# A fused top-k attention and GELU MLP: the last rows' turned probabilities go through VectorE and DRAM, their products with v move later, and the small loads of v change queue

## The chip, the cores and the metric

The kernel runs on one core of a Trainium2 chip. The metric is the device time of one execution in microseconds (us). Three runs of the kernel before took 1480.41, 1480.58 and 1481.08 us (median 1480.58). Engines are named as in the profile: PE (TensorE matmul), PEld (its weight loads), DVE (VectorE), ACT (ScalarE), POOL (GpSimd), SP (SyncE, which here only issues DMAs).

## The reference

Eight batches, eight heads, 576 rows, head size 64, float32. Every row of scores keeps its 32 largest entries; softmax over those; product with v. The heads side by side form x (4608 tokens by 512), and an MLP with an exact GELU follows.

```python
scores = scale * np.matmul(q, k.transpose(0, 1, 3, 2))
kth = np.partition(scores, -top_k, axis=-1)[..., -top_k:-top_k + 1]
scores = np.where(scores >= kth, scores, -1000000000.0)
attn = np.exp(scores - np.max(scores, axis=-1, keepdims=True))
attn = attn / (np.sum(attn, axis=-1, keepdims=True) + 1e-09)
x = np.matmul(attn, v)                      # (B,H,S,D), then to (B*S, H*D)
h = x @ w_in
out = (0.5 * h * (1.0 + erf(h / sqrt(2)))) @ w_out
```

## The kernel before

**Items.** Heads are taken in pairs. An item is 128 rows of scores for both heads of a pair: a tile `s` of 128 partitions and 1152 columns (two heads of 576). A head has 576 = 4 x 128 + 64 rows, so four full row tiles (t = 0 to 3) and 64 last rows (t = 4, `NM`). An item of last rows takes 64 rows of two heads of two pairs. A batch has 16 full items and two of last rows; even batches put their last rows behind their full items, odd batches before them. So four items of last rows stand together at each border between an even and an odd batch: items 16 to 19, 52 to 55, 88 to 91 and 124 to 127 of 144.

**Slots.** The loop `for n in range(ahead)` (L1154) writes the order of every engine out by hand. In slot n: the scores of items n+2 and n+3 on PE in even slots (L386, L401) and their copies from PSUM by ACT (L394, L406); the scores against the last 64 keys, "keys", one item a slot (L349, L363, copied by ACT at L357, L369); the 32 largest of item n on DVE (`top_k`, L483, L486); the selection and the exponentials of item n-1 on ACT (`softmax`, L517, L529), its sum (L510, POOL), reciprocal (L504, DVE, the last DVE instruction of the slot) and scaling (L552, POOL); the turning of P, the scaled probabilities, of item n-2; and the product with v (`attend`) of item n-3 at the slot's start on PE, whose result ACT copies to `xT` (L720 for full items, L731 for last rows). Between these `mlp` puts pieces of the MLP on PE: first-layer pieces (`h_ps`, L773) in even slots, second-layer pieces (`seven`, L927, and `y_ps`, L929) in odd slots, after the GELU (L789) of the pieces before. The GELU and the exponentials use different tables, so an odd slot has two table loads on ACT.

**Two ways to turn P.** On PE: `tails` (L622 for last rows, L619 for others) and `both` (eight transposes, L649) into PSUM, then ACT copies (L635 twice for last rows, L629 for others; L664). Or, for items where `squared(i)` holds (48 even full items): DVE turns all 32 x 32 squares in place in the middle of `top_k` (`square_p`, L569), SP writes the tile to DRAM with four DMAs at the end of the slot (`write_p`, L579), and at the start of the next slot SP reads it back, rearranged, with four DMAs into the left half of `pt` (`read_p`, L586) once the writes have landed.

**Buffers and waits.** `pt`, the turned P of two items side by side, is one buffer. The score tile `s` has six buffers, so item i+6 takes that of item i once the turning has read it. From slot START + 3 on (START is 10) every `bank(...)` is the same single PSUM bank "z": `o` (the product with v), `seven` and the keys use it in turn, and each must wait for the ACT copy of the one before. All loads and stores of the main part go through SP, in order; `issue` holds loads of v back behind `write_p` when the slot has one. In the built program each DMA gets one of eight completion semaphores in turn, whichever queue issues it, and the issuing engine first waits until the DMA that had this semaphore last has landed.

The loads of v of the next batch (`load("v", ...)`, L737) follow the product of the items that used the buffers last: each pair has two loads of 128 KB over 128 partitions (L131) and two of 16 KB over 64 partitions (L134).

Of the kernel before, what the change touches and what calls it, by code (L numbers as in the profile page):

```python
# [14 lines left out]
def kernel(  # L15
# [30 lines left out]
    NP = H // 2  # L46
    NM = S // P
# [51 lines left out]
    def issue(f):  # L99

        if held[0]:
            late_issues.append(f)
        else:
            f()
# [232 lines left out]
    def halves(t, e, step):  # L337

        return spread(t[:, e * TL :], step + (TL if e == 0 else -TL), TL)

    def pair_tile(name, tag="pr"):
        return ps.tile([P, 2, 512], f32, tag=tag, bufs=1, name=name)

    def last_keys(i, t_ps):

        pair, t = items[i]
        s = S_of[i]
        if t < NM:
            nc.tensor.matmul(  # L349
                t_ps[:, 0:P], lhsT=q_of[pair][:, t * P : (t + 1) * P],  # L350
                rhs=kt_of[pair][:, SM : SM + P], start=True, stop=True,
            )
# [4 lines left out]
            return lambda: nc.scalar.activation(  # L357
                s[:, SM : S + TL], t_ps[:, 0:P], func=AF.Copy, scale=scale
            )
        for r in range(2):  # L360
            kt = kt_of[pair + r]
            for e in range(2):
                nc.tensor.matmul(  # L363
                    t_ps[half(r, e), r * TL : (r + 1) * TL],
                    lhsT=kt[:, SM + P + e * TL : SM + P + (e + 1) * TL],
                    rhs=kt[:, SM + e * TL : SM + (e + 1) * TL],
                    start=True, stop=True,
                )
        return lambda: nc.scalar.activation(  # L369
            s.rearrange("p (r n) -> p r n", r=2)[:, :, SM:S],  # L370
            t_ps[:, 0:P].rearrange("p (r n) -> p r n", r=2), func=AF.Copy, scale=scale,
        )

    def scores(i, second=False):
        if i >= N or i in S_of:
            return
        pair, t = items[i]
        S_of[i] = s = work.tile([P, 2 * S], f32, tag="s", bufs=6, name="s")
        s_ps = pair_tile("s_ps", "l1" if second else "pr")
        if not few[0]:  # L380
            last_keys(i, bank("t_ps"))()
        if t < NM:
            q_t, kt = q_of[pair][:, t * P : (t + 1) * P], kt_of[pair]
            for e in range(2):
                rows = slice(e * D, (e + 1) * D)
                nc.tensor.matmul(  # L386
                    s_ps[:, e], lhsT=q_t[rows, :], rhs=kt[rows, 0:SM], start=True, stop=True
                )
            if i == 0:

                nc.scalar.activation(s[:, 0:SM], s_ps[:, 0], func=AF.Copy, scale=scale)
                nc.scalar.activation(s[:, S + TL :], s_ps[:, 1], func=AF.Copy, scale=scale)  # L392
                return
            nc.scalar.activation(spread(s, S + TL, SM), s_ps, func=AF.Copy, scale=scale)  # L394
        else:

            for r in range(2):
                kt = kt_of[pair + r]
                for e in range(2):
                    rows = slice(e * D, (e + 1) * D)  # L400
                    nc.tensor.matmul(  # L401
                        s_ps[half(r, e), r, :], lhsT=kt[rows, SM + P + e * TL : SM + P + (e + 1) * TL],
                        rhs=kt[rows, 0:SM], start=True, stop=True,
                    )
            s2 = s.rearrange("p (r n) -> p r n", r=2)
            nc.scalar.activation(s2[:, :, 0:SM], s_ps, func=AF.Copy, scale=scale)  # L406

    lists_of = {}
    HS = S // 2
# [171 lines left out]
    def read_p(i):  # L581

        if squared(i):
            d = turned.pop(i)
            for k in range(P // SQ):
                nc.sync.dma_start(  # L586
                    out=pt_now[0][k * SQ : (k + 1) * SQ, :, 0:P], in_=d[:, :, k, :]
                )

    def transposes(i):  # L590
# [3 lines left out]
        if squared(i):  # L594

            def keys_only(ahead):
                pt_now[0] = work.tile([P, 2 * NM + 1, 2 * P], f32, tag="pt", bufs=1, name="pt")
# [7 lines left out]
        def tails(ahead):  # L605
            tp = bank("tp_t")
            keys = last_keys(ahead, tp) if ahead is not None and ahead < N else None
            at = P
            if t % 2 == 0:
                pt_now[0] = work.tile([P, 2 * NM + 1, 2 * P], f32, tag="pt", bufs=1, name="pt")  # L610
            if diag is not None:
                for e in range(2):
                    nc.tensor.matmul(
                        tp[e * TL : (e + 1) * TL, at : at + P],
                        lhsT=s[:, SM + e * TL : SM + (e + 1) * TL], rhs=diag[:, e],
                        start=True, stop=True,
                    )
            elif t < NM:
                nc.tensor.transpose(tp[:, at : at + P], s[:, SM : S + TL], ident)  # L619
            else:  # L620
                for r in range(2):
                    nc.tensor.transpose(  # L622
                        tp[0:TL, at + r * P : at + (r + 1) * P],
                        s[:, r * S + SM : (r + 1) * S], ident,
                    )
            if keys:
                keys()
            if t < NM:
                nc.scalar.copy(  # L629
                    out=pt_now[0][:, NM, t % 2 * P : (t % 2 + 1) * P], in_=tp[:, at : at + P]  # L630
                )
                return
            for e in range(2):
                c = slice(e * TL, (e + 1) * TL)
                nc.scalar.copy(  # L635
                    out=halves(pt_end[c, 0, :], e, P),
                    in_=halves(tp[0:TL, at : at + 2 * P], e, P),
                )

        x = t % 2 * P if t < NM else 0  # L640

        def turn_over(tp, e):
            first = e * (S + TL if t < NM else S)
            for j in range(NM):
                to, part = tp[:, j * P : (j + 1) * P], s[:, first + j * P : first + (j + 1) * P]
                if diag is not None:
                    nc.tensor.matmul(to, lhsT=part, rhs=diag[:, e], start=True, stop=True)
                else:
                    nc.tensor.transpose(to, part, ident)  # L649
# [33 lines left out]
    def copy_x():  # L683
        while copies:
            copies.pop()()
# [10 lines left out]
    def attend(i):  # L696
# [24 lines left out]
        else:  # L721
            for r in range(2):
                vt = raw_of("v", pair + r)
                for j in range(NJ):
                    for e in range(2):
                        nc.tensor.matmul(
                            o[e * D : (e + 1) * D, r * TL : (r + 1) * TL], lhsT=vt[:, j, e, :],
                            rhs=pt[:, r * NJ + j, half(r, e)] if j < NM else pt_end[:, r, half(r, e)],
                            start=(j == 0), stop=(j == NJ - 1),
                        )  # L730
            copies.append(lambda: nc.scalar.copy(  # L731
# [588 lines left out]
```

## Time and profile before

| | us |
|---|---|
| median of three runs | 1480.58 |
| the profiled execution's own time | 1479.73 |
| its span in the profile | 1478.0 |
| PE busy | 1461.6 |
| DVE busy | 1294.3 |
| POOL busy | 1140.1 |
| ACT busy | 1099.9 |

Busy times are sums over the whole span, and say little on a single slot: with 144 items in 1478.0 us a slot takes about 10 us, and its limit changes from slot to slot. Slots are best cut at the reciprocal (L504) that ends a slot on DVE. In the profile a matmul in float32 shows as two instructions, so "x8" is four matmuls of the program, and successive start times tell more of PE than busy times do, since matmuls overlap.

### The profile page before, as it was taken

The numbers are of one execution on the slowest core, as the hardware profiler recorded it, in microseconds if no ns is written. First come the engines' busy times: TensorE is split into PE (matmuls) and PEld (weight loads), VectorE is DVE, ScalarE is ACT, GpSimd is POOL, SyncE is SP. The second block draws the span as 40 slices with busy tenths as digits, with TensorE's granted clock in tenths as the row PEclk, the third lists the DMA queues.
The fourth block names the chain that finished last, engine by engine and source line by source line (L and its number), as shares of the span: only waits on it lengthen the run. The fifth ranks groups of instructions, "written<-read, shape, count | busy, mean of one in ns | idle before, by whom it ended". The sixth has DMA issues, their size and how long they took to land. (4 is left out here: it accounts for less than half of the span.)

```text
span 1478.0 us, 27006 instructions
## 1 busy us (share of the span) xinstructions
PE 1461.6 (99%) x8817; PEld 1147.9 (78%) x8817; DVE 1294.3 (88%) x3318; ACT 1099.9 (74%) x1942; POOL 1140.1 (77%) x1291
## 2 busy tenths in 40 slices
PE   8999999999999999999999999999999999999999
PEld 6876677877777777887777778787777777787787
DVE  8999899999999988999999987999999997998701
ACT  7999977877777687777777778777777777776620
POOL 6877567877898879877898978886788887987732
PEclk9999999999999999999999999999999999999999
DMA  7424310045435322345534331345453421233300
GB/s 198 143 86 124 84 48 1 24 88 101 95 73 93 66 58 52 65 95 108 105 83 81 69 61 47 66 93 99 97 103 73 89 55 41 61 61 72 70 15 15
DMA packets 477645, 112.94 MB, mean 76 GB/s; under 512 B 413216, under 2 KB 469056, under 8 KB 477504
## 3 DMA queue, kind: packets, MB, share of 16 engines
q1 hardware_dynamic: 476240, 110.78, 35.3%
q8 instruction: 70, 1.15, 0.3%
q14 instruction: 71, 0.58, 0.1%
q10 hardware_dynamic: 1200, 0.39, 0.1%
q0 software_dynamic: 64, 0.03, 0.0%
HBM read 73.39 MB, written 37.75 MB: 75 GB/s over the span
## 5 line engine op out<-in xcount | busy, mean ns | idle before, releaser
L773 PE MATMUL h_ps<-xT,w_in_sb 128*128 128x256 f32 (+1 forms) x2560 | 536.2, 361 | 0.1
L773 PEld LDWEIGHTS h_ps<-xT,w_in_sb 128*128 128x128 f32 x2560 | 436.5, 190 | 73.4 <-issue 25.2
L483 DVE MAX8 top<-lists 128x8 f32<-128x576 f32 (+1 forms) x792 | 476.4, 641 | 0.0
L486 DVE MATCH_REPLACE8 lists<-top,lists 128x288 f32<-128x288 f32 (+1 forms) x528 | 307.9, 589 | 0.0
L552 POOL TENSOR_TENSOR s<-s,rden 128x1152 f32<-128x1152 f32 x135 | 285.8, 2117 | 0.3 <-DVE rden L504 0.3
L529 ACT ACTIVATE s<-s,bias 128x576 f32<-128x576 f32 x288 | 225.4, 787 | 11.0 <-issue 0.4
L517 ACT ACTIVATE s<-s,neg 128x576 f32<-128x576 f32 x288 | 225.5, 793 | 1.7 <-POOL neg L497 1.6
L510 POOL TENSOR_SCALAR den<-den 128x2 f32<-128x2 f32 x144 | 31.4, 218 | 215.9 <-ACT s L529 210.2
L455 POOL TENSOR_TENSOR lists<-lists 128x576 int32<-128x576 int32 x132 | 186.2, 1410 | 4.0
L447 POOL TENSOR_TENSOR lists<-s 128x576 int32<-128x576 int32 x133 | 187.2, 1407 | 0.0
L715 PE MATMUL o<-pt,raw_v 128*64 128x256 f32 x1280 | 153.0, 384 | 1.8 <-ACT s L529 1.1
L715 PEld LDWEIGHTS o<-pt,raw_v 128*64 128x64 f32 x1280 | 87.8, 136 | 85.8 <-issue 37.2
L789 ACT ACTIVATE g<-h_ps 128x512 f32<-128x512 f32 x144 | 78.2, 594 | 100.6 <-PE h_ps L773 100.4
L929 PE MATMUL y_ps<-w_out_sb,sum 128*128 128x256 f32 x472 | 140.4, 379 | 0.0
L394 ACT ACTIVATE s<-s_ps 128x1024 f32<-128x1024 f32 x127 | 125.5, 1035 | 10.5 <-PE s_ps L386 10.3
L664 ACT COPY pt<-tp 128x1024 f32<-128x1024 f32 x85 | 86.6, 1019 | 62.2 <-PE tp L649 62.1
L386 PE MATMUL s_ps<-kt,qm 64*128 64x512 f32 x512 | 129.4, 618 | 0.8 <-ACT s L392 0.8
L504 DVE RECIPROCAL rden<-den 128x2 f32<-128x2 f32 x144 | 23.2, 161 | 108.6 <-POOL den L510 107.4
L486 DVE MATCH_REPLACE8 lists<-first,lists 128x288 f32<-128x288 f32 x264 | 114.3, 439 | 0.0
L929 PE MATMUL y_ps<-w_out_sb,g 128*128 128x256 f32 x480 | 113.4, 379 | 0.0
L483 DVE MAX8 first<-lists 128x8 f32<-128x288 f32 x268 | 106.6, 436 | 0.0
L929 PEld LDWEIGHTS y_ps<-w_out_sb,g 128*128 128x128 f32 x480 | 91.2, 190 | 12.4
(167 smaller groups left out, 2533.1 us busy)
## 6 DMA issues: line engine op xcount, KB each, us to landing
turned<-s SPq DMA_DIRECT2D x192, 144.0 KB, 3.5
pt<-turned SPq DMA_DIRECT2D x192, 144.0 KB, 3.2
raw_v<-in_v_dram SPq DMA_DIRECT2D x64, 128.0 KB, 2.4
out_dram<-y SPq DMA_DIRECT2D x30, 256.0 KB, 2.1
raw_q<-in_q_dram SPq DMA_DIRECT2D x112, 64.0 KB, 2.0
raw_k<-in_k_dram SPq DMA_DIRECT2D x112, 64.0 KB, 2.0
w_out_sb<-in_moe_w_in_dram SPq DMA_DIRECT2D x14, 511.8 KB, 4.8
w_out_sb<-in_moe_w_out_dram SPq DMA_DIRECT2D x10, 511.8 KB, 4.1
```

The lines of the kernel that those rows point to most:

```text
L386: nc.tensor.matmul(s_ps[:, e], lhsT=q_t[rows, :], rhs=kt[rows, 0:SM], start=True, stop=True)
L394: nc.scalar.activation(spread(s, S + TL, SM), s_ps, func=AF.Copy, scale=scale)
L447: nc.gpsimd.tensor_tensor(t[:, :, 1].bitcast(i32), a.bitcast(i32), b.bitcast(i32), op=ALU.add)
L455: nc.gpsimd.tensor_tensor(into_of(i)[:, :, 1].bitcast(i32), both, top, op=ALU.subtract)
L483: nc.vector.max(x[:, e], src[:, e])
L486: nc.vector.match_replace(dst[:, e], x[:, e], src[:, e], LOWEST)
L517: nc.scalar.activation(s, s, func=AF.Prelu, bias=st["neg"][:, e : e + 1], scale=1.0, alpha=STEEP)
L529: nc.scalar.activation(s, s, func=AF.Exp, bias=st["bias"][:, e : e + 1], scale=1.0, accum_out=st["den"][:, e : e + 1],)
L552: nc.gpsimd.tensor_tensor(s, s, wide, op=ALU.mult)
L715: nc.tensor.matmul(o[e * D : (e + 1) * D, 0:n], lhsT=vt[:, j, e, :], rhs=pt[:, e * NJ + j if j < NM else NM, :], start=(j == 0), stop=(j = ...
L773: nc.tensor.matmul(h_tile(u)[:, i, :], lhsT=w_in_sb[:, ko, f * P : (f + 1) * P], rhs=xT[:, ko, c0 : c0 + n], start=(ko == 0), stop=(ko == ...
L929: nc.tensor.matmul(acc[names][:, k], lhsT=lhsT, rhs=rhs, start=(j == 0 and k == 0), stop=(j == FT // 2 - 1 and k == 1),)
```

## The change

Items of last rows beyond item 26 (52 to 55, 88 to 91, 124 to 127: twelve items) are turned by DVE squares and DRAM, like the even full items. Two such items share one `pt`, left and right half. Their tails and their heads are laid out in `s` as in a full item (both heads' last columns side by side in the middle), so that items 16 to 19, which are still turned on PE, need one transpose and one copy for the tails instead of two and two; `pt_end` goes. The product of an even item of an even batch (52) moves from the start of slot 55 to the start of slot 56; those of 53, 54 and 55 move from the starts of slots 56, 57 and 58 to the middle of slots 57, 59 and 59, ahead of the slot's keys, and `read_p` of that slot moves behind them. The two 16 KB loads of v of each pair that follow these products are issued by ACT instead of SP: eight DMAs at each border, four at the end of slot 56 and four at the end of slot 57.

```diff
         for e in range(2):
                 nc.tensor.matmul(
-                    t_ps[half(r, e), r * TL : (r + 1) * TL],
+                    t_ps[half(r, e), e * TL : (e + 1) * TL],
...
                     nc.tensor.matmul(
-                        s_ps[half(r, e), r, :], lhsT=kt[rows, SM + P + e * TL : SM + P + (e + 1) * TL],
+                        s_ps[half(r, e), e, :], lhsT=kt[rows, SM + P + e * TL : SM + P + (e + 1) * TL],
...
-            nc.scalar.activation(s2[:, :, 0:SM], s_ps, func=AF.Copy, scale=scale)
+            nc.scalar.activation(spread(s, S + TL, SM), s_ps, func=AF.Copy, scale=scale)
...
-    pt_end = const.tile([P, 2, P], f32, name="pt_end")
-    nc.gpsimd.memset(pt_end, 0.0)
 
     def squared(i):
 
-        return SINGLE.stop - 2 < i < N - 2 and i % 2 == 0 and items[i][1] < NM and i % RINGS != 12
+        if not SINGLE.stop - 2 < i < N - 2:
+            return False
+        return items[i][1] == NM or (i % 2 == 0 and i % RINGS != 12)
+
+    def delayed(i):
+
+        return squared(i) and items[i][1] == NM
+
+    def pt_tile():
+        return work.tile([P, 2 * NM + 1, 2 * P], f32, tag="pt", bufs=1, name="pt")
...
         if squared(i):
             d = turned.pop(i)
+            if i % 2 == 0:
+                pt_now[0] = pt_tile()
+            cols = slice(i % 2 * P, (i % 2 + 1) * P)
             for k in range(P // SQ):
                 nc.sync.dma_start(
-                    out=pt_now[0][k * SQ : (k + 1) * SQ, :, 0:P], in_=d[:, :, k, :]
+                    out=pt_now[0][k * SQ : (k + 1) * SQ, :, cols], in_=d[:, :, k, :]
                 )
...
-                            rhs=pt[:, r * NJ + j, half(r, e)] if j < NM else pt_end[:, r, half(r, e)],
+                            rhs=pt[:, e * NJ + j if j < NM else NM, i % 2 * P :][:, half(r, e)],
...
-                issue(lambda r=r: load("v", pair + r + NP))
+                issue(lambda r=r: load("v", pair + r + NP, None, nc.scalar if delayed(i) else None))
...
         held[0] = n < N and squared(n - 2)
-        read_p(n - 3)
+        mid = [i for i in (n - 5, n - 4) if delayed(i) and n % 2 and (i % 2 or i in starts)]
+        if not mid:
+            read_p(n - 3)
...
-        product = attend(n - 3)
+        if delayed(n - 4) and n % 2 == 0 and n - 4 not in starts:
+            product = attend(n - 4)
+        else:
+            product = not delayed(n - 3) and attend(n - 3)
...
         mlp(1)
+        if mid:
+            for i in mid:
+                attend(i)
+                copy_x()
+            read_p(n - 3)
```

More of the change, by code (lines that the diff above doesn't have):

```diff
@@ L335, in half @@
         return slice((r ^ e) * TL, ((r ^ e) + 1) * TL)
-    def halves(t, e, step):
-        return spread(t[:, e * TL :], step + (TL if e == 0 else -TL), TL)
     def pair_tile(name, tag="pr"):
@@ L369, in last_keys @@
         return lambda: nc.scalar.activation(
-            s.rearrange("p (r n) -> p r n", r=2)[:, :, SM:S],
-            t_ps[:, 0:P].rearrange("p (r n) -> p r n", r=2), func=AF.Copy, scale=scale,
+            s[:, SM : S + TL], t_ps[:, 0:P], func=AF.Copy, scale=scale
         )
@@ L401, in scores @@
                     nc.tensor.matmul(
-                        s_ps[half(r, e), r, :], lhsT=kt[rows, SM + P + e * TL : SM + P + (e + 1) * TL],
+                        s_ps[half(r, e), e, :], lhsT=kt[rows, SM + P + e * TL : SM + P + (e + 1) * TL],
                         rhs=kt[rows, 0:SM], start=True, stop=True,
                     )
-            s2 = s.rearrange("p (r n) -> p r n", r=2)
-            nc.scalar.activation(s2[:, :, 0:SM], s_ps, func=AF.Copy, scale=scale)
+            nc.scalar.activation(spread(s, S + TL, SM), s_ps, func=AF.Copy, scale=scale)
     lists_of = {}
@@ L596, in keys_only @@
             def keys_only(ahead):
-                pt_now[0] = work.tile([P, 2 * NM + 1, 2 * P], f32, tag="pt", bufs=1, name="pt")
                 if ahead is not None and ahead < N:
@@ L608, in tails @@
             at = P
-            if t % 2 == 0:
-                pt_now[0] = work.tile([P, 2 * NM + 1, 2 * P], f32, tag="pt", bufs=1, name="pt")
+            if i % 2 == 0:
+                pt_now[0] = pt_tile()
             if diag is not None:
@@ L617, in tails @@
                     )
-            elif t < NM:
+            else:
                 nc.tensor.transpose(tp[:, at : at + P], s[:, SM : S + TL], ident)
[L620 to L625, printed above, removed]
             if keys:
                 keys()
[L628 to L640, printed above, removed]
+            nc.scalar.copy(out=pt_now[0][:, NM, x : x + P], in_=tp[:, at : at + P])
+        x = i % 2 * P
         def turn_over(tp, e):
-            first = e * (S + TL if t < NM else S)
+            first = e * (S + TL)
             for j in range(NM):
@@ L1177 @@
             scores(n + 3)
-        product = attend(n - 3)
+        if delayed(n - 4) and n % 2 == 0 and n - 4 not in starts:
+            product = attend(n - 4)
+        else:
+            product = not delayed(n - 3) and attend(n - 3)
         late = n > START
```

## The prediction

> **What bounds the kernel now.** I read the page first (shares, clock), then stretches of one border cut at the reciprocals that end slots 53 to 59 (the view by windows), then the order of PE, ACT and SP in them.
>
> ```profile
> span 1478.0 us, 27006 instructions
> PE 1461.6 (99%) x8817; PEld 1147.9 (78%) x8817; DVE 1294.3 (88%) x3318; ACT 1099.9 (74%) x1942; POOL 1140.1 (77%) x1291
> PEclk9999999999999999999999999999999999999999
> ```
>
> PE looks like the bound, and its clock never falls. But PE's figure is an average over slots with other limits. The six rows below are slots 54 to 59, where the four items of last rows 52 to 55 are turned and multiplied:
>
> ```profile
> 526.70:536.76 10.06, 10.06 (x63) 8.33 (x60) 8.09 (x23) 6.63 (x13) 9.35 (x11) 1.00 0.07 11
> 536.76:549.07 12.31, 12.31 (x103) 9.53 (x102) 8.09 (x23) 10.27 (x22) 5.91 (x6) 1.00 0.22 50
> 549.07:559.34 10.27, 10.25 (x121) 9.00 (x118) 8.10 (x23) 7.05 (x15) 10.03 (x12) 1.00 0.27 60
> 559.34:569.48 10.14, 10.14 (x54) 7.76 (x53) 8.09 (x23) 9.53 (x17) 9.98 (x12) 1.00 0.14 53
> 569.48:578.75 9.27, 9.27 (x80) 8.30 (x79) 9.27 (x23) 6.62 (x13) 8.66 (x10) 1.00 0.27 42
> 578.75:587.00 8.25, 8.12 (x43) 6.34 (x43) 8.12 (x23) 6.67 (x14) 6.00 (x6) 1.00 0.44 98
> ```
>
> Columns: stretch, its length, then busy time of PE, PEld, DVE, ACT, POOL, then clock and DMA. In slots 56 and 57 POOL is busy 10.03 of 10.27 and 9.98 of 10.14 us: POOL, not PE, sets them, since its sum (L510) stands behind its other work and the reciprocal waits for it. Slot 58 is all DVE (9.27 of 9.27). Only in slots 54 and 55 are DVE (8.09) and POOL both short of the length.
>
> **The change, part by part.** PE's share, from start to start:
>
> ```profile
> 531.68 0.38 PE L622 MATMUL tp_t<-ident,s 128*64 128x128 f32 x2
> 531.89 1.03 PE L773 MATMUL h_ps<-xT,w_in_sb 128*128 128x256 f32 x4
> 532.76 1.04 PE L649 MATMUL tp<-ident,s 128*128 128x128 f32 x8
> 533.63 3.62 PE L773 MATMUL h_ps<-xT,w_in_sb 128*128 128x256 f32 x16
> 537.18 0.69 PE L726 MATMUL o<-pt,raw_v 128*64 128x64 f32 x16
> 538.50 1.13 PE L773 MATMUL h_ps<-xT,w_in_sb 128*128 128x256 f32 x4
> L569 DVE STREAM_TRANSPOSE s<-s 128x1152 f32<-128x1152 f32 x48 | 65.5, 1364 | 0.0
> ```
>
> Tails take 531.89 - 531.68 = 0.21 us, the eight transposes 533.63 - 532.76 = 0.87, one product with v 538.50 - 537.18 = 1.32. So PE is relieved of 1.08 us in each of slots 54 to 57 (4.3 us a border), and DVE gets 1.36 us in each. ACT loses the copies behind them, which hide in its idle time.
>
> Slot 54 becomes 8.09 + 1.36 = 9.45 on DVE, with the wait for POOL 9.6: 0.46 saved. Slot 55 loses its product too: ACT's chain there (10.27 busy) starts earlier and is shorter by the copies, so DVE's 9.45 to 9.5 decides: 2.81 saved. Slots 56 and 57: DVE's 9.45 and PE's smaller load hide under POOL, whose instructions stay the same, end to end up to the sum:
>
> ```profile
> 556.91 0.73 POOL L979 TENSOR_TENSOR y<-y 128x256 f32<-128x256 f32 x1
> 557.59 1.41 POOL L455 TENSOR_TENSOR lists<-lists 128x576 int32<-128x576 int32 x1
> 559.08 0.22 POOL L510 TENSOR_SCALAR den<-den 128x2 f32<-128x2 f32 x1
> ```
>
> Nothing saved there. So at most 3.27 us a border are to be had, not 4.3.
>
> Slot 59 pays. It now holds two products in a row, both in bank z: that of 54 (PE), its copy (ACT), that of 55, its copy, then the keys.
>
> ```profile
> 579.73 0.78 ACT L517 ACTIVATE s<-s,neg 128x576 f32<-128x576 f32 x1 [0.18 <-POOL neg L497]
> 580.57 1.28 ACT L529 ACT_TABLE_LOAD   x1
> 581.87 0.78 ACT L529 ACTIVATE s<-s,bias 128x576 f32<-128x576 f32 x1
> 582.64 0.26 ACT L357 ACTIVATE s<-tp_t 128x128 f32<-128x128 f32 x1
> 581.24 0.41 PEld L349 LDWEIGHTS tp_t<-kt,qm 128*128 128x128 f32 x2
> 587.00 0.17 DVE L504 RECIPROCAL rden<-den 128x2 f32<-128x2 f32 x1
> ```
>
> The first copy stands behind the selection, table load and exponential, which cannot start before slot 58's end: it comes at 582.64 - 578.75 = 3.9 us into the slot however early PE is. Then copy 0.3, product 1.4, copy 0.4: keys at 6.15 instead of 2.5. From the keys to the reciprocal are 5.76 us, 5.45 without a wait of 0.3 there. Slot 59 is then 11.4 to 11.6 instead of 8.25: at least 3.1 lost, which takes back the gain.
>
> The DMAs. Per border 16 writes and 16 reads are new on SP's queue; eight small loads leave it.
>
> ```profile
> 574.82 3.40 SPq L579 DMA_DIRECT2D turned<-s  x4
> 580.89 2.55 SPq L586 DMA_DIRECT2D pt<-turned  x4
> pt<-turned SPq DMA_DIRECT2D x192, 144.0 KB, 3.2
> raw_v<-in_v_dram SPq DMA_DIRECT2D x64, 16.0 KB, 2.3
> L134 SPq DMA_DIRECT2D raw_v<-in_v_dram x64: 465/512/1687, 23.7 to 1249.7; - x64
> L131 ACTq DMA_DIRECT2D raw_k<-in_k_dram x2: 500/525/550, 0.7 to 1.3; - x2
> SPq L134 <- DMA w_out_sb<-in_moe_w_in_dram: 1.8, 2, 1.0
> ```
>
> A write set takes 3.4 us to issue and has landed 580.89 - 574.82 = 6.05 after its first issue (the reads wait for that); a read set 2.55 and 3.2 to land. One load on ACT holds its queue 0.5 us (nearest row: 0.525 for a larger load), four 2.1. The last row shows a load of v waiting for a load it has nothing to do with: the eight semaphores in turn. Here that ties SP to ACT: in the built program the last load of v behind item 52's product takes the semaphore of ACT's first load at the end of slot 57, and the four reads of 54, next on SP, those of its others. So SP stands until ACT is at the end of slot 57, and behind SP's reads of 54 stand the writes of 55. Who waits for those: item 61 takes 55's score buffer, and its scores are copied on ACT at the start of slot 58, in front of everything that slot 58 has on ACT. (Item 59 waits likewise for 53's writes in slot 56, about 1.5 us, under POOL's cover.)
>
> From slot 57's start: exponential at 3.9, product's copy, keys and their copy to 4.7, second selection, second exponential from 5.5 to 6.5. ACT's loads go out under this exponential (5.5) or after it (6.5, and 0.5 later still by the four of slot 56, which push the GELU back). Second load landed: 0.5 + 2.3 later, 8.3; reads of 54 till 11.0; writes of 55 from there, landed 17.1. Slot 58 starts at 10.14, so ACT is held till 6.9 us into it; late end 8.5. Then copy 1.0, selection and exponential twice (1.75 each), keys' copy 0.25, sum and reciprocal 0.5: slot 58 ends at 12.2 to 13.8 instead of 9.27: 3.0 to 4.5 lost. And slot 59's ACT work then begins with the GELU that was held up (table 1.3, GELU 1.05, copy 0.25, begun 0.5 before the slot): first copy at 5.2 instead of 3.9, slot 59 about 12.6: 4.3 lost.
>
> Sum a border: -0.46 - 2.81 + 3.0 to 4.5 + 4.3 = +4.0 to +5.5; nothing in the rows places ACT's loads between these ends, so I take the middle, 4.75. Slot 60 begins as it did, so nothing is made up. Three borders: +14.2. Items 16 to 19 save one tail transpose (0.11, half of 0.21) on PE each, in slots where PE has no idle time: -0.4. The scores' new banks, same instructions: 0, bounds -0.3 and +0.3. Against the profiled execution's 1479.73: 1493.5; the median of the runs stands 0.85 above it: 1494.
>
> **A rule that bears on it.** The Trainium skill, "DMA: Bandwidth & Descriptors", section Issuing engines are not separate DMA queues, says that issuing from several engines saves only the issuing time. By the rows that is eight times 0.5 us of SP, which is not what SP waits for here.
>
> **The rivals.**
> (1) The gain stays, slower falls away: the reads of 54 go out right behind 53's product (SP not held by ACT), and PE, 1.32 us lighter in slot 58, is so far ahead that slot 59's products fit. Then 3.27 x 3 + 0.4 = 10.2 saved: 1470. For it: SP is idle most of the time. Against: the copy at 3.9 us needs DVE's slot 58. It decides if writes of 55 land before slot 58 and the keys of slot 59 come by 3.5 us.
> (2) Only slot 59 pays: -3.27 + 3.2 = 0 a border, 1480. For it: the writes of 55, free of ACT, would land about 2 us into slot 58, in time.
> (3) PE's clock falls. In this schedule PE has done slot 58's first-layer pieces about 7.2 us into the slot and then needs bank z, which the held keys' copy frees at 10.2 to 11.7: PE stands still for 3 to 4.5 us. What a low clock costs:
>
> ```profile
> L1113 PE MATMUL warm<-raw_v 128*128 128x128 f32 x18 | 4.2, 430 | 1.0 <-DVE raw_v L85 1.0
> L1113 PE MATMUL warm<-ident 128*128 128x128 f32 x276 | 32.7, 275 | 0.0
> ```
>
> The first 18 matmuls of the kernel took 430 ns, later ones 275: 1.56 times. On slot 59's path are 3.4 us of PE work (product 1.3, keys to last transpose 2.1), so +1.9 a border: 1500. No clock row of this trace has fallen, so I give it little. The Trainium skill, "TensorE: Matmul & The Clock Gate", Part 1, has the clock halved after an idle window of about 3.4 us; by that the same work would take 3.4 more a border. No run here shows it yet.
> (4) The gain of slot 55 fails (DVE waits for ACT there as now) with all else as forecast: 2.81 x 3 more, 1502.
>
> **How the numbers follow.** Chances: forecast 0.58, (1) 0.14, (2) 0.10, (3) 0.11, (4) 0.07. Time 1494, its own range 1490 to 1498. The range 1479 to 1503 leaves out (1) and a tail. About 0.2% (3 us) is what a measurement of this kernel can tell from no change. Faster 0.14, same 0.10, slower 0.76.
>
> **What the profile after would show.** Right: slots 54 and 55 at about 9.6, slots 56 and 57 unchanged; ACT idle for several us at the start of slot 58 before the scores' copy, ended by the DMA `turned<-s`; SP waiting for a load on ACT's queue before the second half of its loads of v; slots 58 and 59 at 12 to 14 us; PE idle between the two products. Wrong: slot 58 still 9.3 us (the tie of SP to ACT costs nothing), slots 56 and 57 shorter (POOL isn't their limit), or slot 59 near 8.3.

## The result and the profile after

The changed kernel takes 1493.17 us (median of four runs, 1492.42 to 1495.59) against 1480.49 for the kernel before (four runs, 1480.03 to 1481.08): 1.0088 times, interval 1.0071 to 1.0106. It is slower by 12.7 us, and the forecast was 1494 us in a range of 1479 to 1503. The profiled execution took 1492.54 us, its span is 1490.8.

Slot lengths, from reciprocal to reciprocal, in us, with the prediction's term beside the measured change (an own table, worked out from those start times; the three borders hold slots 54 to 59, 90 to 95, 126 to 131):

```
slot   before   after (borders 1, 2, 3)   change          predicted
54     10.06     9.61   9.59   9.60       -0.45 to -0.47  -0.46
55     12.31     9.27   9.27   9.27       -3.04           -2.81
56     10.27    10.49  10.50  10.50       +0.22            0
57     10.14    10.15  10.15  10.15       +0.01            0
58      9.27    12.07  11.93  12.94       +2.7 to +3.7    +3.0 to +4.5
59      8.25    12.48  12.48  12.48       +4.23           +4.3
sum                                       +3.8, +3.6, +4.6  +4.0 to +5.5
```

The same six slots of the first border in the view by windows; columns as before (stretch, length, busy time of PE, PEld, DVE, ACT, POOL, clock, DMA share, GB/s):

```profile
527.20:536.81 9.61, 9.61 (x56) 7.86 (x53) 9.35 (x23) 6.50 (x11) 9.37 (x11) 1.00 0.35 54
536.81:546.08 9.27, 9.27 (x56) 6.96 (x56) 9.27 (x23) 8.42 (x18) 5.91 (x6) 1.00 0.61 124
546.08:556.58 10.50, 10.50 (x78) 9.32 (x75) 9.39 (x25) 6.21 (x12) 10.13 (x12) 1.00 0.66 126
556.58:566.73 10.15, 8.18 (x71) 5.69 (x70) 9.35 (x24) 6.67 (x13) 9.99 (x12) 1.00 0.41 89
566.73:578.80 12.07, 8.52 (x37) 7.13 (x36) 9.35 (x24) 4.58 (x9) 8.65 (x10) 0.92 0.88 205
578.80:591.28 12.48, 11.49 (x122) 9.11 (x122) 8.09 (x23) 8.66 (x17) 5.91 (x6) 0.94 0.56 113
```

Slot 55 is now as long as DVE is busy in it. Slot 57 is still POOL's. In slot 58 no engine is busy for more than 9.35 of 12.07 us: it waits. What it waits for stands in the order of SP and ACT there (start, duration, then in brackets idle time before and what ended it; SPq and ACTq are the issues of DMAs, and "..." marks lines left out):

```profile
557.33 7.00 SPq L131 DMA_DIRECT2D raw_v<-in_v_dram  x4
564.68 3.03 SPq L590 DMA_DIRECT2D pt<-turned  x4
567.81 3.26 SPq L580 DMA_DIRECT2D turned<-s  x4
...
562.04 0.78 ACT L523 ACTIVATE s<-s,bias 128x576 f32<-128x576 f32 x1
562.05 1.12 ACTq L134 DMA_DIRECT2D raw_v<-in_v_dram  x2
...
563.21 1.25 ACTq L134 DMA_DIRECT2D raw_v<-in_v_dram  x2
...
574.08 1.03 ACT L389 ACTIVATE s<-s_ps 128x1024 f32<-128x1024 f32 x1 [8.05 <-DVE lists L480]
```

and, in the view of waits for SP over the border:

```profile
SPq L131 <- DMA raw_v<-in_v_dram: 4.6, 1, 4.6
SPq L580 <- DMA raw_v<-in_v_dram: 3.0, 1, 3.0
```

SP stands 4.6 us inside four of its own loads of v, ahead of the fourth. In the trace this load has the same completion semaphore as the load that ACT issues at 562.05, and it goes out at 563.96; the first three reads of 54 have those of ACT's other three loads. So SP reads 54 at 564.68 and writes 55 at 567.81. (The 3.0 us are the last write of 54, which waits in the same way for ACT's fourth load of slot 56; slot 57 stays as long as it was.) The writes of 55 have landed 6.2 us after the first was issued, and ACT's copy of the scores of item 61, which needs 55's score buffer, starts at 574.08, 7.35 us into the slot. The row names DVE as releaser, but that had long been done. At the second and third border the same row names the DMA, and over the whole span ACT's idle time ahead of these copies has gone from 10.5 us (all but 0.2 put down to PE) to 46.5, of which 21.0, the largest part, are put down to the writes (timeline, then the costliest groups):

```profile
1278.53 1.02 ACT L389 ACTIVATE s<-s_ps 128x1024 f32<-128x1024 f32 x1 [7.98 <-DMA turned<-s]
```

```profile
L389 ACT ACTIVATE s<-s_ps 128x1024 f32<-128x1024 f32 x127 | 125.8, 1032 | 46.5 <-DMA turned<-s 21.0
```

In slot 59 the two products and the keys wait for ACT one after the other (timeline of ACT and PE):

```profile
583.15 0.78 ACT L523 ACTIVATE s<-s,bias 128x576 f32<-128x576 f32 x1
...
583.93 0.24 ACT L718 COPY xT<-o 128x128 f32<-128x128 f32 x1
...
584.23 1.39 PE L713 MATMUL o<-pt,raw_v 128*64 128x64 f32 x40 [0.62 <-ACT xT L718]
585.98 0.49 PE L345 MATMUL tp_t<-kt,qm 128*128 128x128 f32 x2 [0.37 <-ACT xT L718]
```

The first copy comes 5.13 us into the slot, right behind the exponential, the keys 7.18 us into it.

### The profile page after: what moved, and what is told of

Its sections match the earlier page's. It is cut to its first block, busy times and chain, and to the rows that moved or that the text cites. A ratio compares the mean times of both kernels' runs of the same rounds, so it can differ in the third digit from the quotient of the medians.

```text
span 1490.8 us, 26923 instructions
## 1 busy us (share of the span) xinstructions
PE 1452.5 (97%) x8693; PEld 1136.9 (76%) x8693; DVE 1308.9 (88%) x3330; ACT 1082.9 (73%) x1902; POOL 1140.7 (77%) x1290
## 3 DMA queue, kind: packets, MB, share of 16 engines
q8 instruction: 69, 1.13, 0.3%
## 5 line engine op out<-in xcount | busy, mean ns | idle before, releaser
L389 ACT ACTIVATE s<-s_ps 128x1024 f32<-128x1024 f32 x127 | 125.8, 1032 | 46.5 <-DMA turned<-s 21.0
L651 ACT COPY pt<-tp 128x1024 f32<-128x1024 f32 x73 | 74.5, 1020 | 55.9 <-PE tp L636 55.8
```

## The experiments

In each diff, the lines not named are those of the changed kernel unless another base is given. Each comparison is with the kernel before on the same chip (medians 1480.59, 1480.63 and 1480.88 us in the three sets).

### The loads back on SP

```diff
-                issue(lambda r=r: load("v", pair + r + NP, None, nc.scalar if delayed(i) else None))
+                issue(lambda r=r: load("v", pair + r + NP))
```

> The changed kernel with one edit: the small loads of v go back to SP's queue. Tie theory (ACT's loads hold SP by the semaphores in turn, SP's late writes of 55 hold ACT in slot 58): ACT's wait at the start of slot 58 falls from 8 us to at most 2.5 us, slot 58 from 12.1 to 9.4 us, slot 59 from 12.5 to 11.5 us since its GELU is no longer late; 3 x 3.8 = 11 us less, 1482 us. Rival A (slot 59's two products alone are the loss, slot 58 is long because PE and ACT wait for P itself): slots 58 and 59 stay, 1493 us. Rival B (the halved clock is the loss): the two borders with a fall keep it if PE still stands still over 3.4 us.

1484.33 us (1483.07 to 1485.99), 1.0025 times, interval 1.0015 to 1.0035. Slot 58 is 9.27, 9.28 and 9.39 us at the three borders: the loads on ACT's queue made it long. The copy of item 61 still waits 4.73 us, but has run at 569.41, 3.3 us into the slot, under DVE's 9.28. The median is 2.3 us over the 1482 that was expected: slot 59 stays long, 12.94, 11.66 and 12.75, and slots 61, 96 and 97 grow by 0.7, 0.2 and 1.4. The three lengths of slot 59 differ by PE's clock (windows of the first and second border, then PE behind the keys of the first, and of the second):

```profile
575.39:588.33 12.94, 10.76 (x114) 8.46 (x114) 8.13 (x24) 7.43 (x16) 6.01 (x6) 0.87 0.64 134
925.67:937.33 11.66, 9.15 (x115) 7.14 (x115) 8.12 (x24) 7.81 (x17) 6.00 (x6) 1.00 0.65 131
```

```profile
581.36 0.67 PE L345 MATMUL tp_t<-kt,qm 128*128 128x128 f32 x2 [0.39 <-ACT xT L718]
...
583.74 1.63 PE L636 MATMUL tp<-ident,s 128*128 128x128 f32 x8
...
932.03 0.49 PE L345 MATMUL tp_t<-kt,qm 128*128 128x128 f32 x2 [0.39 <-ACT xT L718]
...
933.33 1.04 PE L636 MATMUL tp<-ident,s 128*128 128x128 f32 x8
```

At full clock the slot is 11.66, and the prediction's own figure for a slot 59 whose GELU isn't late was 11.4 to 11.6. Where the clock had fallen, PE took 583.74 - 581.36 = 2.38 us from the keys to the transposes instead of 933.33 - 932.03 = 1.30.

### The loads on ACT alone, in the kernel before

```diff
-                issue(lambda r=r: load("v", pair + r + NP))
+                issue(lambda r=r: load("v", pair + r + NP, None, nc.scalar if t == NM and i > 26 else None))
```

> The kernel before with one part of the change alone: the eight 16 KB loads of v of each border are issued by ACT, the turning and the products stay as they were. Theory (the tie of SP to ACT costs only because reads and writes of the last rows' P stand behind SP's loads): in the kernel before SP has nothing urgent behind them until item 56 is written in slot 58, so the tie costs nothing, and what is left is ACT's own time, 2 us in each of the two slots where the loads stand. Slot 55 (12.31 us, ACT busy 10.27) may take up to 2 us of it, slot 56 is POOL's and hides it: slots 54 to 59 together 0 to 2 us longer than 60.3, median 1480.5 to 1486. Rival (loads on ACT's queue are the loss by themselves): slots 58 and 59 grow by 3 us or more here too, median 1490 or more.

1487.96 us (1486.9 to 1488.78), 1.0051 times, interval 1.0036 to 1.0065. Slots 58 and 59 are as before (9.28, 8.24), so the queue costs nothing there without the reads and writes of the last rows. But slot 55 is 14.83, 14.14 and 14.60 instead of 12.31: 1.8 to 2.5 us more, for up to 2 expected, and the median lies above the expected 1480.5 to 1486. In the timeline of ACT, the copy of 52's product stands behind the four loads; these took 3.11 us, and the copy came at 541.37 instead of 538.64 (slot 55 begins 0.2 us later here):

```profile
538.22 3.11 ACTq L134 DMA_DIRECT2D raw_v<-in_v_dram  x4
541.37 0.27 ACT L731 COPY xT<-o 128x128 f32<-128x128 f32 x1 [4.75 <-DMA raw_v<-in_v_dram]
```

### The scores of item 61 later

```diff
-        two = few[0] and n % 2 == 0 and n + 3 < N and items[n + 3][1] < NM
+        two = few[0] and n % 2 == 0 and n + 3 < N and items[n + 3][1] < NM and not delayed(n - 3)
```

> The changed kernel, loads of v still on ACT, with one edit: the scores of items 59 and 61 (and those 36 and 72 later) are not made in slots 56 and 58 beside those of 58 and 60 but one slot later. SP stays held as before. Tie theory: what hurts is only that item 61's scores' copy stands in front of slot 58's ACT work, so slot 58 falls from 12.1 to about 9.4 us although the writes of 55 land no earlier; slot 59 about 11.5 to 12 us, with one scores' copy more; 1482 to 1485 us. Rival A (ACT's or SP's late loads hurt elsewhere, by the reads of 54 and 55 coming late): slot 58 may fall but the products of slot 59 then wait for the reads of 55, slot 59 13 us or more, 1490 us.

1491.84 us (1489.54 to 1493.96), 1.0074 times, interval 1.0061 to 1.0086. Slot 58 is 9.28 at all borders, as expected where ACT's hold before the selection is the cause: the copy now stands behind the second exponential. But it still waits for the same writes (timeline of ACT, then of PE in slot 59):

```profile
574.01 1.03 ACT L389 ACTIVATE s<-s_ps 128x1024 f32<-128x1024 f32 x1 [3.85 <-DMA turned<-s]
```

```profile
582.60 0.70 PE L345 MATMUL tp_t<-kt,qm 128*128 128x128 f32 x2 [0.35 <-ACT xT L718]
...
585.02 1.59 PE L636 MATMUL tp<-ident,s 128*128 128x128 f32 x8
```

Slot 59 grows to 13.89, 14.40 and 14.50. So of the 2.7 to 3.7 us won in slot 58, 1.4 to 2.0 come back one slot later, and the median is near the 1490 of the rival and not the theory's 1482 to 1485. At the first border it is not the chain up to the keys that grows: the keys come 6.91 us into slot 59, in the changed kernel 7.18. It is PE's clock, which is at 0.50 from 582.72 to 586.13: from the keys to the transposes PE takes 585.02 - 582.60 = 2.42 us, in the changed kernel 587.28 - 585.98 = 1.30. The clock falls at all three borders. At the second and third the product of 55 also waits for its reads, 1.96 and 2.56 us, as the rival had it. So the place of the copy made slot 58 long; SP's lateness stays, and is paid in slot 59.

### POOL's additions left out in slots 56 and 57

The base is the kernel with the loads back on SP; the additions in place of `trio_piece` and `seven_piece` go through a function:

```diff
+    def add_up(y, a, b, op):
+        if slot[0] > 26 and slot[0] % RINGS in (20, 21):
+            return
+        nc.gpsimd.tensor_tensor(y, a, b, op=op)
```

> The changed kernel with all loads of v on SP, and in slots 56 and 57 (and the same two slots of the other borders) the additions in place that gather the MLP's output are left out on POOL: two in slot 56 (1.4 us) and five in slot 57 (3.4 us), so the output is not the reference's there. Theory (POOL sets slots 56 and 57, and hides DVE's added squares): slot 57 falls from 10.15 to 9.3 to 9.6, which is DVE's own work, slot 56 from 10.50 to 9.3 to 9.8. Rival (PE or ACT sets them): both stay within 0.2 us of 10.50 and 10.15. Slots 58 and 59 stay within 0.5 us of 9.27 and 12.94 by both.

Slot 57, where five additions fell away, is 9.28 us at the first two borders and 9.27 at the third, DVE's own work (windows):

```profile
555.99:565.27 9.28, 8.08 (x70) 5.60 (x69) 9.28 (x24) 5.91 (x10) 6.55 (x7) 1.00 0.64 145
```

So POOL set slot 57. Slot 56 stayed at 10.48, but says nothing: its two additions are issued in the turn of the loop before and were still there (POOL 10.12). That slot 56 is POOL's is read from the trace alone: there POOL's instructions follow each other with no gap over 0.1 us from the first up to the sum. The one run took 1484.27 us, no less than with the additions; slot 59 grew (13.42, 12.18 and 13.82 us).

### Products at the slot starts, one PSUM tile for both

Two changes of slot 59 on the kernel with the loads back on SP. In the first, the products of 54 and 55 share one PSUM tile, and are copied after both:

```diff
+        if delayed(i) and i in starts:
+            both_o[0] = bank("o")
+            o = both_o[0]
+        elif delayed(i) and i - 1 in starts:
+            o = both_o[0][:, 2 * TL :]
...
-                copy_x()
+            while copies:
+                copies.pop(0)()
```

> Loads of v on SP as in the run with that edit alone, and the products of 54 and 55 written side by side into one tile of the bank, both copied after both. Theory (slot 59 is long because the second product waits for the copy of the first, which stands behind the exponential 3.9 us into the slot): keys of slot 59 about 1.5 us earlier, slot 59 about 10 instead of 11.5 us, 3 x 1.5 = 4.5 us less than with the loads on SP alone, 1477 to 1478 us. Rival (PE has not enough lead, the products themselves are what the slot lacks): no change against the loads on SP alone.

1484.86 us (1482.93 to 1487.76), 1.0032 times, interval 1.0021 to 1.0043. Slot 59 falls to 10.57, 10.53 and 10.71, as expected. At the second border, where the clock had not fallen with two tiles either, the wait between the products was worth 1.1 us; the 2.4 and 2.0 at the others hold the fallen clock too. Yet the median is no better than with two tiles, since slots 60 and 61 grow (12.35 and 10.58 at the first border, in the kernel before 9.60 and 9.21). There the product of 56 and 57, full items, waits for its reads, and then takes 4.07 us where it took 2.38 with two tiles, since the clock is at 0.50 from 589.38 to 592.79 (timeline of PE and SP):

```profile
573.36 2.84 SPq L590 DMA_DIRECT2D pt<-turned  x4
576.32 3.34 SPq L580 DMA_DIRECT2D turned<-s  x4
583.89 2.54 SPq L590 DMA_DIRECT2D pt<-turned  x4
...
589.13 4.07 PE L710 MATMUL o<-pt,raw_v 128*64 128x256 f32 x20 [2.37 <-DMA pt<-turned]
```

SP comes to the reads of 55 only at 573.36, behind the writes of 55 and eight loads of v; the writes of 56 stand behind those, and the reads of 56 behind their landing. SP carries its lateness on.

In the second, each product of 53 to 55 goes back to a slot's start:

```diff
-        mid = [i for i in (n - 5, n - 4) if delayed(i) and n % 2 and (i % 2 or i in starts)]
+        behind_o = delayed(n - 4) and n % 2 == 1
...
-        if delayed(n - 4) and n % 2 == 0 and n - 4 not in starts:
+        if delayed(n - 4):
             product = attend(n - 4)
...
+        if behind_o:
+            read_p(n - 3)
...
```

> Loads of v on SP, and all four products moved out of the middles: 52, 53, 54, 55 at the starts of slots 56, 57, 58, 59, one product a slot, their copies ahead of the selection and exponential on ACT; the reads of 54 and 56 follow the products of 53 and 55 at once. Theory (a border has 3.2 us to give in slots 54 and 55, and only slot 59's chain takes it back): slot 59 between 8.3 and 9.9 us as PE brings its lead with it, 0 to 1.6 us lost there, so 1.6 to 3.2 us a border gained, 1471 to 1476 us. Rival (POOL and DVE hold slots 56 to 58 so that PE's lead is lost before slot 59): slot 59 9.9 us, 1476 us. If PE's time decided throughout, 4.3 us a border would come out, 1468 us.

1495.21 us (1493.19 to 1496.76), 1.0093 times, interval 1.0078 to 1.0109, outside of what was expected. Slot 59 is 17.82, 15.73 and 17.27. The product of 55, at the slot's start, finds no P, and stops PE with all that is queued behind it; then the clock is at 0.50 from 578.94 to 585.77. SP issues the reads of 55 only at 573.96:

```profile
579.60 2.40 PE L713 MATMUL o<-pt,raw_v 128*64 128x64 f32 x40 [4.50 <-DMA pt<-turned]
```

The middle of the slot had hidden SP's lateness. I had left SP's own time out of that expectation.

### Only the even items squared

52 and 54 go by DVE and DRAM, 53 and 55 are turned on PE into the right half, both products of a pair stand at the starts of slots 56 and 58 in one PSUM tile, and all loads of v are on SP. Three orders of SP: all sixteen loads behind the writes of 54, all ahead of them, and eight on either side. The core of the edit, and the line that splits the loads:

```diff
-        return items[i][1] == NM or (i % 2 == 0 and i % RINGS != 12)
+        return i % 2 == 0 and i % RINGS != 12
...
+        if i % 2 and t == NM and squared(i - 1):
+            both_o[0] = bank("o")
+            attend_last(i - 1, both_o[0])
+            held[0] = squared(i + 1)
+            attend_last(i, both_o[0][:, 2 * TL :])
+            return True
```

> Only the even items of last rows (52, 54) go by DVE squares and DRAM; the odd ones (53, 55) are turned on PE into the right half of the same tile, as with full items. Both products of a pair follow each other at the start of slot 56 (52, 53) and slot 58 (54, 55) in one PSUM tile, and all loads of v are on SP, behind the writes of 54. Theory (what the changed kernel loses lies in slots 58 and 59, in SP's order and in products behind an exponential; what it gains lies in slot 55): slot 54 9.6, slot 55 9.3 to 10.9 instead of 12.31, slots 56 and 57 10.1 to 10.8 (POOL), slot 58 9.3 to 10, slot 59 8.2 to 8.8; 1.5 to 3.3 us less a border, median 1470 to 1476. Rival (SP's single queue is late again): the reads of 54 stand behind eight loads of v and reach the product of slot 58 2 us late: slot 58 11 to 12 us, the gain of slot 55 is spent, median 1479 to 1484.

> As the kernel in which only the even items of last rows are squared, with one difference in SP's order: the eight loads of v behind the products of 52 and 53 go out at once in slot 56, ahead of the writes of 54. Theory: the reads of 54 are in time in both, median within 1.5 us of the other, slots 56 to 59 within 0.3 us each. Rival (SP is late in the other): slot 58 is 1.5 to 3 us shorter here than there, median 5 to 9 us lower than there. A third outcome: the loads hold back the writes of 54, these free a buffer late, and slot 57 or 58 here is longer than there by over 1 us.

> Only the even items of last rows are squared, both products of a pair at the start of slots 56 and 58, all loads of v on SP, and their order on SP split: the loads behind 52's product go out at once in slot 56, those behind 53's product behind the writes of 54. From the two kernels that had all sixteen loads on one side of these writes: loads from 546.9, eight of them 4.5 us, writes of 54 as soon as the squares are done (551.3 to 554.6), eight loads to 559.2, reads of 54 to 561.7, landed at 565, when slot 58's product asks for them. Theory (slot 58 only lost because SP brought 54 late): slot 58 falls to 9.3 to 10.3 and slot 59, whose lateness came out of slot 58, to 8.3 to 9.5; a border 1 to 3.5 us shorter than before, median 1470 to 1477. Rival (two products at the start of slot 58 are too much for PE whatever SP does): slot 59 stays at 10.6 and slot 58 over 9.8, median 1479 to 1484.

Loads behind: 1491.96 us (1490.81 to 1492.91), 1.0075 times, interval 1.0063 to 1.0087. Loads ahead: 1487.23 (1482.72 to 1489.95), 1.0041, interval 1.0029 to 1.0054. Split: 1475.42 (1474.43 to 1478.17), 0.9967, interval 0.9956 to 0.9979. Nothing but SP's order differs, and slot 58 is 15.14, 14.20, 14.40, then 12.31, 10.77, 13.02, then 9.28 at all three borders. Slot 59 is 10.59 in the first two, and 9.41, 9.66 and 10.14 in the third, up to 0.6 over what was expected. My theory for the first of these was wrong by over 15 us: I had put the loads at eight and 5 us of SP, and they are sixteen (eight for each of 52 and 53). With all of them behind the writes, from 555.15 to the reads at 564.98, they take 9.83 us, and 54's P comes when PE has long been waiting (SP, then PE). With all of them ahead, the writes of 54 wait, its reads go out at 562.98, and PE waits 3.85 us. Loads behind:

```profile
555.15 0.68 SPq L131 DMA_DIRECT2D raw_v<-in_v_dram  x1
...
564.98 2.57 SPq L590 DMA_DIRECT2D pt<-turned  x4
...
570.34 4.54 PE L699 MATMUL o<-pt,raw_v 128*64 128x64 f32 x80 [5.46 <-DMA pt<-turned]
```

With them split, the reads go out at 561.14 and PE waits 1.13 us (the row names a store, but in the trace the last of these reads has landed at 566.47, just ahead of the product). The two products take 2.55 us here and 4.54 above, where the clock is at 0.50 from 569.46 to 576.29, so a part of the difference is the clock's:

```profile
561.14 2.57 SPq L590 DMA_DIRECT2D pt<-turned  x4
...
566.60 2.55 PE L699 MATMUL o<-pt,raw_v 128*64 128x64 f32 x80 [1.13 <-DMA out_dram<-y]
```

### One item squared, and none

> No last rows by DVE and DRAM: all four items of a border are turned on PE as before (one tail transpose and one copy each), but both products of a pair stand at the start of slots 56 and 58 in one PSUM tile, as in the kernels in which only the even items were squared. Theory (slot 55's 3 us come from the product of 52 leaving the slot, not from PE's or DVE's lighter turning): slot 54 10.06, slot 55 9.3 to 10, slot 56 10.3 to 11.6, slot 57 10.15, slot 58 9.3 to 10.6, slot 59 8.25; a border 0.4 to 3 us shorter than before, median 1471 to 1479. Rival (PE's whole work sets the border, and what leaves slot 55 comes back in slots 56 and 58): slots 54 to 59 together within 0.5 us of 60.3, median 1479 to 1482.

> Only the first item of each border (52, 88, 124) is squared; the other three are turned on PE; products in pairs at the start of slots 56 and 58. No read or write of last rows stands on SP after slot 55, so SP cannot make slots 58 and 59 late. Theory: slot 54 9.6, slot 55 9.3, slot 56 10.3 to 11.6, slot 57 10.15, slot 58 9.3 to 10.6, slot 59 8.25; a border 1 to 3.5 us shorter than before, median 1470 to 1478. Rival (PE's whole work sets the border): 1 us shorter at most, which is the one turning that PE loses, median 1477 to 1481.

The core of the edit on the split order, with the items beyond 26 of last rows in pairs as there:

```diff
-        return i % 2 == 0 and i % RINGS != 12
+        return i % 2 == 0 and i % RINGS != 12 and items[i][1] < NM
```

and for the first item of each border alone `(items[i][1] < NM or i not in starts)`. None squared: 1475.55 us (1475.22 to 1476.71), 0.9965 times, interval 0.9953 to 0.9978. The first alone: 1472.45 (1472.1 to 1473.22), 0.9943, interval 0.9931 to 0.9956: the fastest, 8.4 us below the kernel before. Windows of slots 54 and 55 with none squared, then of slots 54 to 59 with the first alone:

```profile
527.00:536.95 9.95, 9.95 (x62) 8.22 (x59) 8.09 (x22) 6.71 (x13) 9.34 (x11) 1.00 0.09 14
536.95:546.83 9.88, 9.88 (x52) 8.02 (x52) 8.10 (x23) 9.34 (x20) 5.91 (x6) 1.00 0.01 2
```

```profile
526.81:536.40 9.59, 9.59 (x56) 7.83 (x53) 9.35 (x23) 6.49 (x11) 9.35 (x11) 1.00 0.36 55
536.40:545.65 9.25, 9.25 (x49) 7.47 (x49) 8.09 (x22) 8.37 (x19) 5.92 (x6) 1.00 0.36 84
545.65:556.60 10.95, 10.95 (x126) 9.48 (x123) 8.09 (x22) 7.31 (x15) 10.03 (x12) 1.00 0.41 94
556.60:566.75 10.15, 10.15 (x68) 7.82 (x68) 8.10 (x23) 9.30 (x16) 9.98 (x12) 1.00 0.21 69
566.75:576.03 9.28, 9.28 (x105) 8.38 (x100) 9.28 (x24) 5.71 (x11) 8.65 (x10) 1.00 0.27 43
576.03:584.56 8.53, 8.53 (x46) 6.86 (x46) 8.12 (x24) 7.11 (x14) 6.00 (x6) 1.00 0.41 95
```

Slot 55 falls from 12.31 to 9.88 without a single square: 2.43 of its 3.04 us come from 52's product leaving the slot, with the one tail transpose and copy that fall away. Squares are worth 0.36 in slot 54 (9.95 to 9.59) and 0.63 in slot 55. Part of what left comes back in slot 56 (10.95 instead of 10.27) and slot 59 (8.53 instead of 8.25), in both kernels, so the six slots sum to 58.7 us with no item squared and 57.8 with one, before 60.3. PE, full in nearly all of these slots, is not a bound that merely shifts its work about.

## Why the prediction was right, and where not

- Slots 54 and 55: right in place and nearly in size, -3.50 for -3.27 a border. For slot 55 the prediction named the product that leaves and ACT's chain made shorter by the copies, without parting them; the kernel with no item squared shows that the product, with one tail transpose and copy, is most of it. (A transpose is one instruction in the profile, unlike other matmuls in float32: "x8" of L649 is eight transposes, as the prediction counts them.)
- Slots 56 and 57: right. POOL sets slot 57 (shown). The +0.22 of slot 56 was not foreseen, and lies in POOL's first two small instructions. In the kernel before, slot 55 ended on POOL's sum, and from the reciprocal to POOL's scaling it was 549.92 - 549.07 = 0.85 us; now slot 55 ends on DVE, which has 53's squares, and it is 547.15 - 546.08 = 1.07. From the scaling to the next sum POOL takes 9.16 and 9.17 us. With only the even items squared slot 55 ends on POOL's sum again, and slot 56 is 10.27.
- Slot 58: the mechanism is right in each step that was named: SP's wait for a load on ACT's queue (4.6 us), the writes of 55 behind it, the copy of item 61 held till 7.35 us (third border 8.22) into the slot, for 6.9 to 8.5 forecast. Putting the loads back on SP took the whole term away. It was sized too high, 2.7 to 3.7 us for a middle of 3.75, but not for the copy: at 7.35, 7.21 and 8.22 us it came about where the middle has it, 7.7. ACT's loads went out under the exponential at all three borders (562.05 beside 562.04), the early end of what was forecast; at the third that exponential began 6.7 us into slot 57 instead of 5.4 to 5.5. What was too large is the chain behind the copy: from its start to the slot's end 4.72 us, for 1.0 + 3.5 + 0.25 + 0.5 = 5.25.
- Slot 59: +4.23 for +4.3; first copy 5.13 us into the slot for 5.2, end 12.48 for 12.6. (Two steps of the working are 0.15 too high: 3.9 + 0.3 + 1.4 + 0.4 is 6.0 and not 6.15, and 8.3 + 2.55 is 10.85 and not 11.0.)
- Items 16 to 19: the -0.4 is there, slots 19, 20 and 21 became shorter by 0.21, 0.11 and 0.11 us. The six-slot sums make 3.8 + 3.6 + 4.6 = +12.0 us and all slots together +12.3, the medians +12.7. That the time comes out within 1 us of the forecast is in part luck: of each border, 0.23 more saved in slots 54 and 55 and 0.22 lost in slot 56 cancel.
- Rival (2), only slot 59 pays, is what happens with the loads back on SP: slot 58 does not pay then. The writes of 55 let the copy of item 61 go 3.3 us into the slot, for the 2 of the rival. At the border where the clock did not fall the six slots do come out near zero, 60.47 for 60.30: slot 59 costs 3.4 there. At the others it costs 4.5 and 4.7, and slots 60 and 61 are late at two borders, hence 1484.33 and not 1480.
- Rival (3), PE's clock, came true as an event and not as a price. At the first two borders PE stood idle for 3.55 and 3.77 us and the clock fell; at the third it stood for 3.48 and the clock stayed. Slot 59 is 12.48 at all three (windows of slot 59 at borders 2 and 3), because there PE waits for ACT's exponential:

```profile
930.51:943.00 12.49, 11.44 (x122) 9.07 (x122) 8.09 (x23) 8.74 (x17) 5.91 (x6) 0.95 0.59 113
1283.25:1295.73 12.48, 10.00 (x118) 7.88 (x119) 8.09 (x22) 8.66 (x17) 5.90 (x6) 1.00 0.57 112
```

  The price is set by what stands on the path: nothing here, and 1.1 to 1.3 us in the kernel with the loads back on SP (12.94 and 12.75 against 11.66). PE's work from the keys to the transposes was 2.38 / 1.30 = 1.83 times as long there, not 1.56 times.

  The Trainium skill, "TensorE: Matmul & The Clock Gate", Part 1, has the clock halved after an idle window of about 3.4 us. The trace agrees in the changed kernel: at the first border the windows below have PE busy for 0.10 of 3.41 us, and then the clock at 0.50 for 3.41. It doesn't agree with the loads back on SP, where the clock fell at 581.52 though PE's longest stop there was 1.69 us: in the 3.41 us before PE was busy for 1.55 (the last two rows, of which the first shows the stop).

```profile
573.38:576.79 3.41, 0.10 (x1) 0.00 (x0) 2.70 (x5) 2.62 (x6) 1.90 (x2) 1.00 0.96 267
576.79:580.20 3.41, 3.17 (x8) 2.57 (x9) 1.40 (x4) 3.35 (x6) 1.58 (x4) 0.50 0.95 225
928.36:931.77 3.41, 3.03 (x7) 2.52 (x8) 1.26 (x4) 3.35 (x7) 1.44 (x4) 0.50 1.03 233
1276.52:1279.94 3.42, 1.48 (x7) 0.95 (x5) 3.14 (x7) 1.41 (x2) 2.34 (x3) 1.00 0.93 185
1279.94:1283.35 3.41, 1.87 (x9) 1.69 (x10) 0.10 (x2) 3.27 (x8) 0.27 (x2) 1.00 1.01 300
```

```profile
579.58 1.39 PE L713 MATMUL o<-pt,raw_v 128*64 128x64 f32 x40 [1.69 <-ACT xT L718]
578.11:581.52 3.41, 1.55 (x41) 1.41 (x42) 3.41 (x12) 1.67 (x5) 3.23 (x3) 1.00 1.03 160
```

  A low stretch lasts 3.41 us or twice that, and within a trace the stretches begin whole multiples of 3.413 us apart (928.36 - 576.79 = 351.57 is 103 times). So the clock goes by windows that are fixed in time. The stop of 3.48 us lay across two such windows, with PE busy for 1.48 us of one and 1.87 of the other. Counted in this way over all traces, without their first 40 and last 10 us, PE was busy for at most 1.55 us in the 18 windows ahead of a fall, and for at least 1.47 in every full-clock window without one. PE's busy times are modelled, so the limit is no sharper than that.

- Rival (1), the gain stays, failed on slot 59's exponential, the point that spoke against it: with SP free of ACT the first copy still came 579.28 - 575.39 = 3.89 us into the slot, for 3.9. Its saving of 10 us was nearly there to be had in another order: 8.4 with one item squared. Rival (4) did not come about: slot 55 is 9.27.
- What the prediction did not see: SP's issuing time as a limit of its own. It counted the reads and writes and found SP idle most of the time, but sixteen loads of v at one border are nearly 10 us in a row, and whatever stands behind them on the queue is late by that.

## What to carry to other kernels

A queue that issues DMAs in order is an engine of its own: count its issuing time in the stretch where a late buffer is needed, and place urgent reads and writes between long rows of loads (the same DMAs in three orders gave 1491.96, 1487.23 and 1475.42 us). Moving a few small loads to another engine's queue can make it worse, since DMAs that share completion semaphores tie the two queues together. Before giving work to another engine, try moving it by a slot: here moving one product, with one tail transpose and copy less, took about 1.6 us off a border, and taking one item's turning off PE 0.8 to 1.0 more.

## What the runs showed of the hardware that was not expected

- Four 16 KB loads on ACT held the instruction behind them for 3.1 us in one place (the kernel before with the loads on ACT), where 2.1 had been worked out from single issues; issued under a running exponential, two took 1.12.
- PE's clock fell without a long stop of PE: with the loads back on SP it fell at the first border though no stop of PE there was longer than 1.69 us, since PE was busy for only 1.55 of the 3.41 us before. A stop of 3.48 us in the changed kernel, across two such windows, left it as it was. A fall has to be read border by border, not from the span's mean (0.998).
